# The leaky activation of the first three segments, written in place in its PSUM bank

## The chip, the cores and the metric

The kernel runs on one core of one Trainium2 chip. The metric is the device time of one execution in microseconds (us), lower is better. Engines are named as the profile names them: PE (TensorE matmul), PEld (its weight loads), DVE (VectorE), ACT (ScalarE), POOL (GpSimd), SP (SyncE, which here only issues DMAs).

## The reference, cut to what matters

A decayed linear attention produces `x` of 3072 tokens by 512. Two feed-forward layers follow, each 512 to 2048 to 512; the first has a leaky activation, the second `h * cos(h)`:

```
h = x @ w_in                       # 3072x512 @ 512x2048
g = np.maximum(0.01 * h, h)
x = g @ w_out                      # 3072x2048 @ 2048x512
h = x @ w_in2 ;  g = h * np.cos(h) ;  out = g @ w_out2
```

The change touches only the way from `h` to `g` of the first layer.

## The kernel before

**Numbers in two parts.** Every float32 operand of a matmul is held as a high part, rounded to the matmul's input format, and a low part, the rest. A product is three matmuls that add up in one PSUM bank (`mm3`, lines 361 to 364): high by high, low by high, high by low. So each intermediate is split: a copy on ACT makes the high part (`high_g`, line 568), a subtraction on DVE makes the low part (`low_g`, line 572).

**Tiling of the first layer.** Tokens come in six blocks of 512. The hidden width of 2048 comes in 16 chunks `f` of 128. For one block and one chunk, `gemm1` (line 550) makes one *product* `hp`: 12 matmuls into one whole PSUM bank of 128 by 512 float32. `Leaky.begin` (line 558) applies the leaky activation (Prelu on ACT, line 560) and writes it to the tile `t` in SBUF, of which there are two. `high_g` and `low_g` read `t` and write the pair `g` (three buffers). `gemm2_a` (line 782) then adds `g` times the second weight into four accumulators `acc`: 12 matmuls more. This text calls them the *accumulation* of that product.

**Segments.** The weights of the first layer have to be rounded on the chip before use, so the first two blocks are cut into four segments: block 0 chunks 0 to 6, block 1 chunks 0 to 3, block 0 chunks 7 to 15, block 1 chunks 4 to 15; then blocks 2 to 5 whole. The first three segments have 7 + 4 + 9 = 20 products; this text numbers them 0 to 19 in their order, and product 20 is the first of the fourth segment.

**Banks.** Products rotate through a pool of two PSUM banks (`ps_h`, `bufs=2`): product i takes the bank of product i-2. The accumulators hold four banks, attention the other two.

**The order of work** is written out by hand in the loop over `f` and kept by every engine's queue. In the iteration of product i come: `gemm1` of i on PE; `high_g` of i-1 on ACT; steps of attention (`slots`); perhaps a *rounding step* of the weights (`tick(0)`); the accumulation of product i-3 on PE (`second`), with the copies out of the accumulators where a segment ends; `low_g` of i-1 on DVE; the Prelu of i on ACT; attention again; perhaps a second rounding step (`tick(1)`).

A rounding step (`Weights.pieces`) is on ACT two activations (lines 121, 123) and a copy (line 142); on DVE a clamp (line 126), a shift (line 129), a bit merge (line 134) and the subtraction of the low part (line 145); on POOL one addition (line 139). `TICKS` says how many steps, none to two, an iteration gets. Attention's part on DVE is mostly the masking of scores (`sf`, line 489) and the scaling of its result (lines 524 and 528).

```
    ps_h = ctx.enter_context(tc.tile_pool(name="ps_h", bufs=2, space=PSUM))
...
        return tmp.tile([P, BLK], F32, tag=tag, name=tag, bufs=4 if tag == "o" else 2)
```

Of the kernel before, what the change touches and what calls it, by code (L numbers as in the profile page):

```python
# [81 lines left out]
def body(ctx: ExitStack, tc: tile.TileContext, att, w1, w2, tab, out):  # L82
# [19 lines left out]
    def stage(tag="o"):  # L102
        return tmp.tile([P, BLK], F32, tag=tag, name=tag, bufs=4 if tag == "o" else 2)
# [43 lines left out]
    class Weights:  # L147
# [52 lines left out]
        def tick(self):  # L200

            self.step()
            while self.run:
                self.step()
# [31 lines left out]
    def flush():  # L236
        for out, in_ in late:
            nc.sync.dma_start(out=out, in_=in_)
        del late[:]
# [112 lines left out]
    def load_wi(p, place):  # L352
        assert ("p", p) in made
        for old in [o for o in wi if wi[o][1] == place]:
            del wi[old]
        t = xpool.tile([P, 4096], F32R, tag=f"b{place}", name=f"b{place}")
        wi[p] = t, place
        for lo, hi in ((0, 1024), (1024, 2048), (2048, 3072), (3072, WIN)):
            nc.sync.dma_start(out=t[:, lo:hi].bitcast(F32), in_=w2i[p][:, lo:hi])
# [190 lines left out]
    def gemm1(key, f, x, hp):  # L550
        w = wslot[key, f, 0]
        xh, xl = x
        for k in range(KD):
            mm3(hp, w[:, k * P : k * P + P], w[:, 512 + k * P : 512 + k * P + P], xh[:, k, :], xl[:, k, :], k == 0, k == KD - 1)


    class Leaky:
        def begin(self, hp):
            t = stage("t")
            nc.scalar.activation(out=t, in_=hp, func=AF.Prelu, alpha=0.01)  # L560
            return (t,)

# [3 lines left out]
    def high_g(g, pair=None):  # L566
        pair = pair or gpool.tile([P, 2, BLK], F32R, tag="g", name="g")
        nc.scalar.copy(out=pair[:, 0], in_=g)  # L568
        return pair

    def low_g(g, pair, eng):
        eng.tensor_tensor(out=pair[:, 1], in0=g, in1=pair[:, 0].bitcast(F32), op=ALU.subtract)  # L572
        return pair

    with tc.manual_schedule():

        with ExitStack() as pctx, ExitStack() as actx:
# [70 lines left out]
            def half(f):  # L648
                nonlocal m, turn
                t = own(2 + turn % 2)  # L650
                turn += 1
                first, mid, last = rounding(raw2, t)
                high, low = parts(t, w2d[f], 0, nc.gpsimd, False, ostage)
                for i, step in zip((0, 2, 3, 3, 4, 5), (begin(f, 1), first, mid, last, high, low)):
                    agenda.put(m + i, step)
                agenda.put(m + 5, done("w", f))
                m += 3
# [25 lines left out]
            def pair(p):  # L683
                nonlocal m, turn
                t1, t2 = own(2 + turn % 2), own(3 - turn % 2)
                fetches = [begin(2 * p + i, 0) for i in range(2)]
                times = (0, 2, 3, 3, 3, 5, 6, 6, 4, 5, 7, 8, 8, 9, 9, 10, 10)
                pair_at(agenda, m, p, t1, t2, (raw2, raw2), fetches, times, (nc.gpsimd, nc.gpsimd, nc.vector), ostage, ostage, True)
                m += 9
# [8 lines left out]
            def last_pairs(ppool):  # L698
                def room(tag, n, dt, bufs):
                    return ppool.tile([P, n], dt, tag=tag, name=tag, bufs=bufs)  # L700

                def pout(n):
                    return room("po", 512, F32, 3)[:, :n]

                for i, p in enumerate(range(OWN, NF // 2)):
                    t1, t2 = late_fn(partial(room, "t1", 512, I32, 3)), late_fn(partial(room, "t2", 512, I32, 3))
                    raws = [late_fn(partial(room, "raw", 1024, I32, 3)) for _ in range(2)]
                    fetches = [lambda raw=raw, f=2 * p + j: fetch2(raw(), f, 0) for j, raw in enumerate(raws)]
                    times = (-2 if i else 0, 2, 3, 4, 1, 4, 5, 6, 5, 6, 7, 8, 8, 9, 9, 10, 10)
                    pair_at(agenda, LAST + 6 * i, p, t1, t2, raws, fetches, times, (nc.gpsimd, nc.gpsimd, nc.vector), pout, ostage)  # L710
# [8 lines left out]
            def load_w(n):  # L719
                for at in loads[:n]:  # L720
                    wa.load(*at)
                del loads[:n]

            def need(w, f, part):
                while (w.key, f, part) not in wslot:
                    load_w(1)
                    w.tick()
# [83 lines left out]
            def second(limit):  # L811
                while len(pending) > limit:
                    fn, *args = pending.pop(0)
                    fn(*args)
# [5 lines left out]
            leaky = Leaky()  # L820
            for seg, (n, f0, f1) in enumerate(SEGMENTS):
                limit = LAG - 2 if seg < 4 else 1
                steps = list(PLAN[seg])
                size, at = len(steps), 0

                def slots(k):
                    for _ in range(size - len(steps), min(size, (k * size + size // 2) // (2 * (f1 - f0)))):
                        steps.pop(0)()

                def tick(k):  # L830
                    if seg < 4 and wa.busy() and k < int(TICKS[seg][f - f0]):
                        if loads and (seg > 0 or loads[0][0] < NF - 7):
                            load_w(1)
                        wa.tick()
                    if n > 1:
                        flush()
                        agenda.run(2 * (NF * (n - 2) + f - START) + k)

                for f in range(f0, f1):
                    if n == NB - 1 and f % 4 > 1:  # L840
                        hp = ps_att.tile([P, 512], F32, tag="attA" if f % 4 == 2 else "attB", name="hp")
                    else:
                        hp = ps_h.tile([P, 512], F32, tag="h", name="hp")
                    hp = hp[:, :BLK]
                    if len(pending) > limit:
                        need(wa, pending[0][2], 1)
                    need(wa, f, 0)
                    gemm1("a", f, xs[n], hp)
                    if n == NB - 1 and f == 8:
                        load_wi(0, 0)  # L850
                    if n == NB - 1 and f == NF - 1:
                        load_wi(1, 1)
                    if prev:
                        g = leaky.finish(*begun)
                        gh = high_g(g)
                    slots(2 * (f - f0) + 1)
                    tick(0)
                    second(limit)
                    if prev:
                        pending.append((gemm2_a, *prev[:2], low_g(g, gh, nc.vector), *prev[2:]))  # L860
                    begun = leaky.begin(hp)
                    slots(2 * (f - f0) + 2)
                    tick(1)
                    prev = n, f, f0, f1
                if f1 == NF:
                    xs.pop(n)
                if n == NB - 2:
                    actx.close()
                    ppool = pctx.enter_context(tc.tile_pool(name="ppool", bufs=1))
                    last_pairs(ppool)  # L870
# [124 lines left out]
        for q in range(QUADS):  # L995
# [12 lines left out]
            if q == 0:  # L1008
                t = leaky.finish(*begun)
# [69 lines left out]
```

## Time and profile before

| | us |
|---|---|
| median of 3 runs | 1144.34 (1143.41 to 1146.3) |
| the profiled execution's own time | 1144.19 |
| its span in the trace | 1142.4 |
| PE busy in the span | 1118.1 (98%) |
| DVE busy in the span | 829.5 (73%) |

The profiled execution lies within 0.15 us of the median, and its span 1.8 us below its own time. The page's chain of the work that ended last puts 84% of the span on PE and 8% on DVE. The shares of the whole span say little on the first 160 us, in which the first three segments lie: there DVE is as full as PE, and the views by stretch and in order of time are needed. In them a row's duration counts from the start of an instruction to its end; neighbours on one engine overlap by some 0.08 us, and the matmuls of a product start every 0.23 us though each is shown at 0.39 us.

### The profile page before, as it was taken

Reading aid. Unit: us, or ns where it says so; the run is one execution under the profiler, and the core shown is the slowest. Engines: PE = TensorE matmul, PEld = TensorE weight load, DVE = VectorE, ACT = ScalarE, POOL = GpSimd, SP = SyncE. Lnnn points to the kernel's source line nnn. Section 1 sums busy time; section 2 is a strip of 40 time slices with the busy share of each in tenths; the row PEclk is TensorE's granted clock in tenths of the full one; section 3 lists DMA queues with packets and bytes.
Section 4 is the critical chain, followed back from the end, with each engine's and each line's share of the span. In section 5 each row is a group of like instructions: output and inputs, shape, how many; then the busy total and the mean of one; then the engine's idle time right before and its main releaser. Section 6 shows DMA issues by size and latency. Waiting matters only on the chain.

```text
span 1142.4 us, 15590 instructions
## 1 busy us (share of the span) xinstructions
PE 1118.1 (98%) x5584; PEld 924.7 (81%) x5584; DVE 829.5 (73%) x1334; ACT 524.9 (46%) x954; POOL 272.0 (24%) x253
## 2 busy tenths in 40 slices
PE   7889999999999999999999989999999999999998
PEld 5678888888888888788888868888888888888886
DVE  7899975344465465655298698798797897867875
ACT  5457643333454444444355445444454453444432
POOL 5455432222344445344166100000000000000000
PEclk9999999999999999999999999999999999999999
DMA  9906422223344444543477456558448366433312
GB/s 342 333 2 219 168 74 74 75 74 119 122 167 156 160 158 153 175 127 107 142 267 299 154 200 209 181 204 314 157 166 285 121 240 230 141 127 139 134 69 75
DMA packets 73806, 190.14 MB, mean 166 GB/s; under 512 B 8192, under 2 KB 12416, under 8 KB 73728
## 3 DMA queue, kind: packets, MB, share of 16 engines
q1 hardware_dynamic: 73584, 188.88, 47.7%
q8 instruction: 44, 0.72, 0.2%
q14 instruction: 34, 0.28, 0.1%
q10 hardware_dynamic: 144, 0.26, 0.1%
HBM read 136.68 MB, written 52.43 MB: 166 GB/s over the span
## 4 chain that ended last, share of the span: by engine, by line
PE 84%; DVE 8%; ACT 3%; DMA 2%; POOL 2%; issue 2%; ACTq 0%; POOLq 0%; DVEq 0%; SPq 0%
PE hp L364 11%; PE hp L362 11%; PE hp L363 10%; PE acc L362 10%; PE acc L363 10%; PE acc L364 10%; PE attB L364 4%; PE attB L362 4%; PE attB L363 4%; PE attA L362 2%; PE attA L364 2%; PE attA L363 2%; PE attA L513 1%; POOL cbuf L139 1%; DVE w L145 1%
## 5 line engine op out<-in xcount | busy, mean ns | idle before, releaser
L362 PE MATMUL acc<-g,w 128*128 128x512 f32 x384 | 151.8, 395 | 0.8 <-DVE o L775 0.8
L364 PE MATMUL hp<-b,w 128*128 128x512 f32 x384 | 150.1, 391 | 1.2 <-POOL b L540 1.1
L362 PE MATMUL hp<-b,w 128*128 128x512 f32 x384 | 150.2, 391 | 0.5 <-ACT b L539 0.5
L363 PE MATMUL acc<-g,w 128*128 128x512 f32 x384 | 149.9, 390 | 0.3 <-DVE w L145 0.3
L363 PE MATMUL hp<-b,w 128*128 128x512 f32 x384 | 149.8, 390 | 0.0
L364 PE MATMUL acc<-g,w 128*128 128x512 f32 x384 | 149.7, 390 | 0.0
L917 ACT ACTIVATE r<-r,bias 128x512 f32<-128x512 f32 x96 | 69.6, 725 | 88.0 <-DVE r L916 88.0
L572 DVE TENSOR_TENSOR g<-t,g 128x512 fp32r<-128x512 f32 x96 | 95.8, 1000 | 16.0 <-ACT g L568 15.4
L362 PE MATMUL hp<-w,b 128*128 128x512 f32 x224 | 87.4, 390 | 0.8 <-DVE c L898 0.8
L363 PE MATMUL hp<-w,b 128*128 128x512 f32 x224 | 87.2, 389 | 0.0
L364 PE MATMUL hp<-w,b 128*128 128x512 f32 x224 | 87.2, 389 | 0.0
L364 PEld LDWEIGHTS hp<-b,w 128*128 128x128 f32 x384 | 72.1, 188 | 17.4 <-POOL b L540 2.5
L362 PEld LDWEIGHTS acc<-g,w 128*128 128x128 f32 x384 | 72.1, 188 | 16.7 <-DVE o L775 1.3
L362 PEld LDWEIGHTS hp<-b,w 128*128 128x128 f32 x384 | 72.1, 188 | 15.7 <-ACT b L539 0.8
L364 PEld LDWEIGHTS acc<-g,w 128*128 128x128 f32 x384 | 72.1, 188 | 15.3
L363 PEld LDWEIGHTS hp<-b,w 128*128 128x128 f32 x384 | 72.1, 188 | 14.5 <-DVE w L145 0.2
L363 PEld LDWEIGHTS acc<-g,w 128*128 128x128 f32 x384 | 72.1, 188 | 14.2 <-DVE w L145 0.6
L457 DVE TENSOR_TENSOR qbd<-raw,qbd 64x256 fp32r<-64x256 f32 x64 | 49.8, 777 | 37.4 <-ACT qbd L456 36.3
L363 PE MATMUL acc<-w,g 128*128 128x512 f32 x192 | 75.1, 391 | 1.1 <-DVE g L572 1.0
L364 PE MATMUL acc<-w,g 128*128 128x512 f32 x192 | 74.8, 389 | 0.0
L362 PE MATMUL acc<-w,g 128*128 128x512 f32 x192 | 74.7, 389 | 0.0
L568 ACT CAST g<-t 128x512 fp32r<-128x512 f32 x96 | 59.3, 618 | 33.3 <-PE acc L364 32.3
(194 smaller groups left out, 2462.9 us busy)
## 6 DMA issues: line engine op xcount, KB each, us to landing
b<-w2i SPq DMA_DIRECT2D x60, 512.0 KB, 5.9
w<-w SPq DMA_DIRECT2D x32, 512.0 KB, 7.7
raw<-att SPq DMA_DIRECT2D x32, 512.0 KB, 4.8
w<-w2d SPq DMA_DIRECT2D x32, 512.0 KB, 7.9
w<-xq SPq DMA_DIRECT2D x28, 512.0 KB, 6.1
cbuf<-w SPq DMA_DIRECT2D x24, 512.0 KB, 3.8
xq<-o SPq DMA_DIRECT2D x40, 256.0 KB, 2.3
w2i<-o SPq DMA_DIRECT2D x32, 256.0 KB, 2.8
```

What stands on the lines that cost most here:

```text
L139: nc.gpsimd.tensor_tensor(out=t, in0=t, in1=raw[:, :, 0], op=ALU.add)
L145: nc.vector.tensor_tensor(out=w[:, 512:1024], in0=t.bitcast(F32), in1=w[:, 0:512].bitcast(F32), op=ALU.subtract)
L362: nc.tensor.matmul(o, sh, mh, start=start, stop=False)
L363: nc.tensor.matmul(o, sl, mh, start=False, stop=False)
L364: nc.tensor.matmul(o, sh, ml, start=False, stop=stop)
L457: nc.vector.tensor_tensor(out=ql[rows, :, cols], in0=rq[rows], in1=qh[rows, :, cols].bitcast(F32), op=ALU.subtract)
L513: nc.tensor.matmul(po[r * D : r * D + D, h // 2, :], d["vp"][:, h, :], s, start=c == 0, stop=c == 0 or h > 1)
L568: nc.scalar.copy(out=pair[:, 0], in_=g)
L572: eng.tensor_tensor(out=pair[:, 1], in0=g, in1=pair[:, 0].bitcast(F32), op=ALU.subtract)
L917: nc.scalar.activation(out=r, in_=r, func=AF.Sin, bias=bias[:, 1:2], scale=1.0)
```

## The change

In the first three segments `Leaky.begin` no longer takes a tile `t` from SBUF: the Prelu writes its result over `hp` in the product's PSUM bank, and `high_g` and `low_g` read it from there. From the fourth segment on nothing changes.

```diff
     class Leaky:
-        def begin(self, hp):
-            t = stage("t")
+        def begin(self, hp, stay=False):
+            t = hp if stay else stage("t")
             nc.scalar.activation(out=t, in_=hp, func=AF.Prelu, alpha=0.01)
             return (t,)
...
-                    begun = leaky.begin(hp)
+                    begun = leaky.begin(hp, seg < 3)
```

No instruction is added, removed or moved on any engine. What differs is operands and waits. On ACT, in the iteration of product 0 (`w_0_166` is attention's result on its way to the block `b`, `hp` the product), the Prelu and the copy of the high part stand where they stood:

```order
 L142 CAST w_0_476<-cbuf 128x512 [waits Pool_49]
 L539 CAST b_508<-w_0_166 128x2x128 [waits DVE_49]
-L560 ACTIVATE t<-hp 128x512 [waits PE_49]
-L568 CAST g<-t 128x512 [waits Activation_49]
+L560 ACTIVATE hp<-hp 128x512 [waits PE_49]
+L568 CAST g<-hp 128x512 [waits Activation_49]
 L539 CAST b_508<-w_0_166 128x2x128 [waits DVE_49]
```

Only the tile has changed. On PE, at the start of product 2 (`w_0_476` is the first weight of chunk 2), behind attention's matmuls:

```order
 L502 MATMUL attB<-w_0_154,st 128x128
 L513 MATMUL attB<-sf,vp 64x128 x4
-L362 MATMUL hp<-b_248,w_0_476 128x512 [waits Activation_49]
+L362 MATMUL hp<-b_248,w_0_476 128x512 [waits DVE_49,Activation_49]
 L363 MATMUL hp<-b_248,w_0_476 128x512
 L364 MATMUL hp<-b_248,w_0_476 128x512
```

The first matmul of product 2 waited for the Prelu of product 0, the last reader of its bank. Now it waits for DVE, and the DVE instruction that the semaphore's value stands for is the subtraction of the low part of product 0. The same holds for products 3 to 20, each with the low part of the product two before. One more thing differs in the built program: product 21, of the fourth segment, is placed in the bank of product 20, where it waits for the Prelu of product 20; before, it had the other bank. From product 22 on the two banks alternate again.

## Rows read from the trace of the kernel before

**Rows 1.** The page, the span:
```profile
span 1142.4 us, 15590 instructions
```
**Rows 2.** Busy time by stretch; columns as the head line says:
```profile
core 0: us, PE busy (x) PEld busy (x) DVE busy (x) ACT busy (x) POOL busy (x), PEclk, DMA share, GB/s
60.00:90.00 30.00, 26.38 (x153) 20.90 (x152) 29.32 (x48) 17.15 (x33) 15.09 (x12) 1.00 0.08 26
90.00:120.00 30.00, 30.00 (x134) 24.85 (x133) 29.36 (x42) 21.92 (x40) 15.45 (x14) 1.00 0.52 186
```
**Rows 3.** Groups between 30 and 160 us: count, busy us, mean ns, idle before:
```profile
L572 DVE TENSOR_TENSOR g<-t,g 128x512 fp32r<-128x512 f32 x19 | 27.4, 1445 | 0.0
L560 ACT ACTIVATE t<-hp 128x512 f32<-128x512 f32 x20 | 11.9, 594 | 2.6 <-DVE g L572 2.6
L489 DVE TENSOR_TENSOR sf<-attA,tb 128x512 f32<-128x512 f32 x9 | 6.2, 688 | 1.2 <-PE attA L486 1.1
```
**Rows 4.** In order of time, POOL and DVE: start us, duration us, engine, line:
```profile
88.05 1.78 POOL L139 TENSOR_TENSOR cbuf<-cbuf,w 128x512 int32<-128x512 int32 x1 [1.55 <-DVE cbuf L134]
88.58 1.81 DVE L572 TENSOR_TENSOR g<-t,g 128x512 fp32r<-128x512 f32 x1
...
95.67 1.80 DVE L572 TENSOR_TENSOR g<-t,g 128x512 fp32r<-128x512 f32 x1
...
147.20 1.64 POOL L139 TENSOR_TENSOR cbuf<-cbuf,w 128x512 int32<-128x512 int32 x1 [2.21 <-DVE cbuf L134]
147.59 0.68 DVE L489 TENSOR_TENSOR sf<-attB,tb 128x512 f32<-128x512 f32 x1
148.19 0.94 DVE L126 TENSOR_SCALAR cbuf<-cbuf 128x512 f32<-128x512 f32 x1
```
**Rows 5.** PE in order of time: products 2, 3, 5, 6, and three waits:
```profile
43.47 0.50 PE L362 MATMUL hp<-b,w 128*128 128x512 f32 x1
...
47.50 1.13 PE L486 MATMUL attA<-w,w 128*128 128x256 f32 x4 [1.01 <-DVE sf L489]
...
49.59 0.50 PE L362 MATMUL hp<-b,w 128*128 128x512 f32 x1
...
56.33 1.13 PE L486 MATMUL attA<-w,w 128*128 128x256 f32 x4 [1.00 <-DVE sf L489]
...
65.60 0.49 PE L362 MATMUL hp<-b,w 128*128 128x512 f32 x1
...
71.89 1.13 PE L486 MATMUL attA<-w,w 128*128 128x256 f32 x4 [3.12 <-DVE sf L489]
...
77.12 0.39 PE L362 MATMUL hp<-b,w 128*128 128x512 f32 x1
```
**Rows 6.** DVE in order of time: low parts 0, 1, 3 and 4:
```profile
46.04 0.68 DVE L572 TENSOR_TENSOR g<-t,g 128x512 fp32r<-128x512 f32 x1
...
53.88 1.80 DVE L572 TENSOR_TENSOR g<-t,g 128x512 fp32r<-128x512 f32 x1
...
69.34 1.77 DVE L572 TENSOR_TENSOR g<-t,g 128x512 fp32r<-128x512 f32 x1
...
80.14 1.79 DVE L572 TENSOR_TENSOR g<-t,g 128x512 fp32r<-128x512 f32 x1
```
**Rows 7.** Products 10 and 11 on PE; DVE's copies as the first segment ends:
```profile
101.21 0.39 PE L362 MATMUL hp<-b,w 128*128 128x512 f32 x1
...
102.86 1.29 DVE L775 COPY o<-acc 128x512 f32<-128x512 f32 x2
...
106.65 0.39 PE L362 MATMUL hp<-b,w 128*128 128x512 f32 x1
```
**Rows 8.** DVE in the iteration of product 13: masking, and low part 12:
```profile
121.17 0.69 DVE L489 TENSOR_TENSOR sf<-attA,tb 128x512 f32<-128x512 f32 x1
...
125.10 0.68 DVE L572 TENSOR_TENSOR g<-t,g 128x512 fp32r<-128x512 f32 x1
```
**Rows 9.** The fourth segment: product 21 on PE, Prelu of product 20:
```profile
165.14 0.39 PE L362 MATMUL hp<-b,w 128*128 128x512 f32 x1
...
166.28 0.59 ACT L560 ACTIVATE t<-hp 128x512 f32<-128x512 f32 x1
```

## The prediction

> **What bounds the kernel now.** I read the span first [rows 1]: 1142.4 us, against 1144.19 us of the execution's own time, so 1.8 us lie around it and are left alone by the change. Next the busy time by stretch [rows 2], because the change ends with product 19, in the first 160 us. In the stretch from 60 us PE lacks 3.6 of 30 us and DVE lacks 0.7; from 90 us on PE is full and DVE still lacks only 0.6. So DVE binds up to about 86 us, and PE behind that, with DVE hard on its heels. The PEclk column is 1.00 in both, the upper of the two levels (2.4 GHz); I expect no price from the clock.
>
> The third view is the groups by line [rows 3]. The subtraction of the low part (L572) has a mean of 1445 ns, while the masking of scores (L489), of the same 128 by 512 elements, has 688. The view in order of time tells why [rows 4]. POOL's addition starts at 88.05 and ends at 89.83; the low part starts at 88.58 and ends at 90.39, some 0.6 us behind POOL: it was held until POOL was done. At 147.59 a masking runs inside a POOL addition (147.20 to 148.84) and takes 0.68 us, unheld. The masking reads one operand from PSUM, the low part reads both from SBUF. The clamp behind the masking, SBUF to SBUF, is held again (0.94 us, ending 0.3 us behind POOL).
>
> The fourth view is PE in order of time beside DVE [rows 5, 6]. It shows when low part i ends and when PE starts product i+2. Before the change those two are strangers. Now the second waits for the first.
>
> **The change part by part.** *Low parts.* After the change the low part reads `hp` from PSUM, as the masking does, so I take 0.68 us for it where it was 1.8. 19 times (1445 - 680) ns are 14.5 us of holding, some 13 low parts at 1.1 us. Not all of it comes back: where the next DVE instruction is a clamp it is held in the low part's place, and ends 0.3 us behind POOL instead of 0.6 + 0.4 behind, a gain of 0.6. Where the next is a masking the whole 1.1 us is gained. The bounds are 0 (held as before) and 1.1; the row at 147.59 is the nearest, as it has the same shape, engine and operands.
>
> *Prelu and high part.* No row shows ACT or DVE writing PSUM. The nearest rows are the Prelu from PSUM to SBUF, 594 ns, and, on the other engine, 688 ns [rows 3]. A tenth of a us either way, 20 times, is at most 2 us if all of it lay on the path; ACT is not on it while DVE is late, so I take 0 and keep 2 us either way for the range. The tile `t` itself cost one wait of 2.6 us on ACT [rows 3], off the path.
>
> *The bank's wait.* Product i+2 must now wait for low part i. On PE nothing passes a waiting matmul: the accumulation behind it and attention's scores are queued there, and DVE waits for those in turn. I work the rows forward [rows 5, 6], carrying PE's delay:
> - Product 2 started at 43.47; low part 0 ends at 46.04 + 0.68 = 46.72. Wait 3.25, delay 3.25.
> - Product 3 started at 49.59, behind a wait of 1.01 for a masking, which is now long done: ready at 49.59 + 3.25 - 1.01 = 51.83. Low part 1 ends at 53.88 + 0.68 = 54.56. Wait 2.7, delay 5.0.
> - The wait of 1.00 at 56.33 goes too: delay 4.0 at product 4, which finds its bank free.
> - Product 5: ready at 65.60 + 4.0 = 69.6; low part 3 ends at 69.34 + 0.68 = 70.0. Wait 0.4, delay 4.4. I give DVE no gain so far: the 1.1 us it saved at low part 1 it spends waiting for the later scores.
> - The wait of 3.12 at 71.89 goes. Product 6: ready at 77.12 + 4.4 - 3.1 = 78.4; low part 4, now 1.1 us earlier by the relief at low part 3, ends at 80.14 - 1.1 + 0.68 = 79.7. Wait 1.3, delay 2.6.
>
> So the first stage costs 7.7 us of waits and gives back 5.1: **+2.6**. Behind it PE was full, and every wait adds whole.
>
> *Ends of segments.* DVE copies two of the four accumulators out, and the next low part is queued behind these copies. Product 10 now waits for low part 8, which waits for the second copy, which waits for PE's last matmul before product 10. That bubble is one copy and one low part: 1.29 / 2 + 0.68 and a tenth for the handing over, **+1.4** [rows 6, 7]. What hid it before was that low part 8 was not due for two more products. In the iteration of product 13 the same queue begins with a masking that waits for PE's scores after product 13. From that masking to the end of low part 12 DVE needs 125.78 - 121.17 = 4.6 us [rows 8], most of it a rounding step. PE has one accumulation to do meanwhile, half of the 5.44 us between products 10 and 11 [rows 7], 2.7 us. **+1.9** at product 14.
>
> *Iterations with two rounding steps.* From 88.58 to 95.67 DVE needs 7.09 us [rows 4], after the relief some 6.5; PE needs 5.44. With no lead DVE makes PE wait 1.0 there, and iterations with one step or none give the lead back. Some four places are of that kind; I put **+0.6** for all, an estimate between 0 and 3.
>
> *The swapped bank.* Product 21 waits for the Prelu of product 20. Before, it started at 165.14, and that Prelu ended at 166.28 + 0.59 = 166.87 [rows 9]. PE and ACT come to this place equally late, so **+1.7**.
>
> The sum is 2.6 + 1.4 + 1.9 + 0.6 + 1.7 = 8.2 us. What comes behind is bound by PE and hides none of it.
>
> Two banks are all that products have, and rows 5 and 6 show PE ready 0.4 to 3.3 us before the low part that now frees one. The Trainium skill ("PSUM — Partial Sum Buffer", Summary: rules for kernel authors) says to evacuate PSUM promptly, which speaks against this change. By that rule alone there would be the waits without relief on DVE, and the time would be that of the third rival below; by rows 4 the relief is real, and the sum stays at 8.2.
>
> **The rivals.**
> *Slower by 8, the forecast*: 1144.2 + 8.2 = 1152.4 us.
> *Faster.* The mechanism is DVE's relief up to 86 us: PE's three waits for the masking (5.1 us) go and the bank is never waited for, 1144.2 - 5.1 = 1139 us. For it speaks that DVE binds there and is held 1.1 us at a time; it decides at the point where low part i ends before PE is ready for product i+2. Against it: at products 2 and 3 the low part is 3.3 and 2.7 us too late, and the relief of low part 0 is nothing (0.68 already).
> *No change to measure.* The first stage costs its 2.6, but then DVE, some 0.6 us per product ahead, keeps a lead through both ends of segments, and Prelu 20 comes earlier too: 1144.2 + 2.6 = 1146.8 us. Against it: at both ends DVE waits for PE's own matmuls, which no lead shortens.
> *Slower by 16.* Reading `hp` is held by POOL like reading `t`: 13 low parts at 0.6 us are not gained, 1152.4 + 7.8 = 1160 us. Against it stands the masking at 147.59.
>
> **How the numbers follow.** About 0.3% (3.4 us) is what a measurement of this kernel tells from no change. Chances: forecast 0.72, faster 0.07, no change 0.14, slower by 16 0.07. The forecast's own range is 1148 to 1158: the 2 us for ACT's writes, 0 to 3 for the double steps instead of 0.6, and a handing over of 0.1 to 0.3 us at each of some eight waits. The whole range adds half of the no-change case below, to 1146; the faster case and the one slower by 16 stay outside. So faster 0.07, the same 0.14, slower 0.79. I predict 1152.5 us; the median of the runs is 0.15 us above the profiled execution, which changes nothing.
>
> **What would show it.** In the profile after: the mean of L572 between 30 and 160 us near 700 ns, and the clamp (L126) held more often. PE idle before products 2, 3 and 6 for some 3, 3 and 1 us with DVE's L572 as releaser, and no more waits of PE for L489 at the places that now read 47.50, 56.33 and 71.89. Near products 10 and 14 PE idle for 1.4 and 1.9 us behind DVE's copies; at product 21 an idle of 1.7 us put down to ACT's Prelu. The prediction is wrong if PE starts product 3 within a us of 49.6, or if L572 keeps durations of 1.8.

## The result, and the profile after

The changed kernel takes 1154.96 us (median of 4 runs, 1154.47 to 1155.44), the kernel before 1144.64 beside it. The ratio is 1.0085, with a 95% interval of 1.0073 to 1.0097: slower by 10.3 us, where 8.2 had been forecast.

The page of after: the span, and the busy time of each engine.

```profile
span 1153.5 us, 15598 instructions
...
PE 1123.8 (97%) x5584; PEld 928.7 (81%) x5584; DVE 818.5 (71%) x1334; ACT 524.2 (45%) x954; POOL 269.7 (23%) x253
```

The span is longer by 11.1 us than that of [rows 1], while DVE works 11.0 us less than before (829.5). The change took work off an engine and lost time all the same. The page counts 8 instructions more in all than [rows 1]; on each engine above the number is that of before.

Busy time by stretch, after, with the columns of [rows 2]:

```profile
30.00:60.00 30.00, 26.05 (x155) 20.87 (x150) 26.80 (x48) 15.78 (x35) 14.87 (x14) 0.89 0.87 298
60.00:90.00 30.00, 27.48 (x172) 22.19 (x171) 24.60 (x46) 15.17 (x29) 13.57 (x11) 1.00 0.09 28
90.00:120.00 30.00, 28.38 (x125) 22.85 (x124) 28.19 (x42) 21.76 (x40) 16.03 (x14) 1.00 0.52 183
120.00:150.00 30.00, 28.04 (x118) 22.51 (x117) 23.95 (x38) 19.00 (x36) 11.09 (x8) 0.94 0.47 158
```

From 60 to 90 us DVE is no longer full: 24.6 us where it was 29.3. From 90 us on PE, which was full, lacks 1.6 us and then 2.0 us in 30. And the granted clock, 1.00 before, is 0.89 and 0.94 in two of these stretches. Of that more below.

Groups by line in the first stages (30 to 167 us), after:

```profile
L126 DVE TENSOR_SCALAR cbuf<-cbuf 128x512 f32<-128x512 f32 x28 | 23.5, 840 | 0.1
...
L572 DVE TENSOR_TENSOR g<-hp,g 128x512 fp32r<-128x512 f32 x19 | 13.0, 684 | 3.4 <-ACT g L568 3.4
...
L560 ACT ACTIVATE hp<-hp 128x512 f32<-128x512 f32 x20 | 11.6, 581 | 7.1 <-PE hp L364 7.1
```

and the clamp before:

```profile
L126 DVE TENSOR_SCALAR cbuf<-cbuf 128x512 f32<-128x512 f32 x29 | 21.9, 754 | 0.2
```

The low part (L572) now takes 684 ns every time, against 1445 in [rows 3]: with one operand in PSUM POOL no longer holds it. The clamp behind it takes 840 instead of 754, so 28 x 0.086 = 2.4 us of the 14.4 that the low parts are spared (27.4 - 13.0) are held again in another place. ACT's writing into PSUM costs nothing that shows: the Prelu takes 581 ns, 594 in [rows 3].

What PE waited for between 30 and 190 us, after (line, releaser: us in total, times, longest):

```profile
PE hp L362 <- DVE g L572: 10.7, 8, 3.6
PE hp L362 <- ACT t L560: 1.6, 1, 1.6
```

No product waited for either before; the three waits for the masking of [rows 5], 5.1 us, are gone.

### The profile page after: what moved, and what is told of

Its sections match the earlier page's. It is cut to its first block, busy times and chain, and to the rows that moved or that the text cites. A ratio compares the mean times of both kernels' runs of the same rounds, so it can differ in the third digit from the quotient of the medians.

```text
span 1153.5 us, 15598 instructions
## 1 busy us (share of the span) xinstructions
PE 1123.8 (97%) x5584; PEld 928.7 (81%) x5584; DVE 818.5 (71%) x1334; ACT 524.2 (45%) x954; POOL 269.7 (23%) x253
## 4 chain that ended last, share of the span: by engine, by line
PE 83%; DVE 8%; DMA 4%; ACT 2%; issue 1%; POOL 1%; SPq 0%; ACTq 0%; DVEq 0%; POOLq 0%
PE hp L362 11%; PE hp L364 11%; PE hp L363 11%; PE acc L362 10%; PE acc L363 10%; PE acc L364 10%; PE attB L364 4%; PE attB L362 4%; PE attB L363 4%; PE attA L362 2%; PE attA L364 2%; PE attA L363 2%; DMA w<-w 1%; DMA w<-att 1%; PE attA L513 1%
## 5 line engine op out<-in xcount | busy, mean ns | idle before, releaser
L362 PE MATMUL hp<-b,w 128*128 128x512 f32 x384 | 152.3, 397 | 12.3 <-DVE g L572 10.7
L364 PE MATMUL hp<-b,w 128*128 128x512 f32 x384 | 151.5, 395 | 0.0
L363 PE MATMUL hp<-b,w 128*128 128x512 f32 x384 | 151.3, 394 | 0.0
L362 PEld LDWEIGHTS hp<-b,w 128*128 128x128 f32 x384 | 72.9, 190 | 30.4 <-issue 6.7
L364 PEld LDWEIGHTS hp<-b,w 128*128 128x128 f32 x384 | 73.1, 190 | 15.8 <-POOL b L540 0.4
L363 PEld LDWEIGHTS hp<-b,w 128*128 128x128 f32 x384 | 73.0, 190 | 14.4
L572 DVE TENSOR_TENSOR g<-t,g 128x512 fp32r<-128x512 f32 x76 | 66.1, 870 | 16.6 <-ACT g L568 16.0
L362 PE MATMUL attB<-w,w 128*128 128x512 f32 x180 | 70.4, 391 | 0.5 <-DVE w L966 0.5
```

The lines of the kernel that those rows point to most:

```text
L362: nc.tensor.matmul(o, sh, mh, start=start, stop=False)
L363: nc.tensor.matmul(o, sl, mh, start=False, stop=False)
L364: nc.tensor.matmul(o, sh, ml, start=False, stop=stop)
```

## Experiments

Each run is compared with runs of the kernel before on the same chip. "Faster" and "slower" below are against their median unless another kernel is named.

**The changed kernel again.** Its first profile had stretches at a lower clock, so I wanted a second one.

> The changed kernel once more, unaltered. Theory (the clock's fall behind the idle of 1.96 us at product 14 is there in some executions and not in others, and costs 0.8 us net, since the small waits behind it take up the rest): 1154.5 to 1155.4 us; if product 14 now takes 3.0 us, products 15 and 17 wait some 0.2 us each instead. Rival (it falls every time in this kernel): product 14 takes 4.4 us again.

1154.98 us (1154.44 to 1155.78), ratio 1.0086 [1.0072, 1.01]. The two runs at a mean granted clock of 0.999 took 1154.45 and 1154.44, the two at 0.994 took 1155.78 and 1155.52. Its profile, of the 1154.45 one, is the cleanest picture of the change and is called the clean one below; only from 30 to 60 us is its granted clock under 1.00, at 0.94. The products at which PE now waits, products 2, 3, 5, 6, 10, 11, 14, 15, 17, 18 and 21, without a wait products 8, 13, 20 and 22, and the last matmul ahead of product 15 (start us, duration us, engine, line, operation, idle before and its releaser):

```profile
47.12 0.77 PE L362 MATMUL hp<-b,w 128*128 128x512 f32 x1 [3.56 <-DVE g L572]
...
54.83 0.47 PE L362 MATMUL hp<-b,w 128*128 128x512 f32 x1 [1.41 <-DVE g L572]
...
70.42 0.47 PE L362 MATMUL hp<-b,w 128*128 128x512 f32 x1 [0.83 <-DVE g L572]
...
80.18 0.47 PE L362 MATMUL hp<-b,w 128*128 128x512 f32 x1 [1.68 <-DVE g L572]
...
92.67 0.39 PE L362 MATMUL hp<-b,w 128*128 128x512 f32 x1
...
105.09 0.50 PE L362 MATMUL hp<-b,w 128*128 128x512 f32 x1 [1.38 <-DVE g L572]
...
111.06 0.50 PE L362 MATMUL hp<-b,w 128*128 128x512 f32 x1 [0.24 <-DVE g L572]
...
122.09 0.39 PE L362 MATMUL hp<-b,w 128*128 128x512 f32 x1
...
130.40 0.50 PE L362 MATMUL hp<-b,w 128*128 128x512 f32 x1 [1.96 <-DVE g L572]
...
135.76 0.39 PE L364 MATMUL acc<-g,w 128*128 128x512 f32 x1
...
136.36 0.50 PE L362 MATMUL hp<-b,w 128*128 128x512 f32 x1 [0.22 <-DVE g L572]
...
147.82 0.47 PE L362 MATMUL hp<-b,w 128*128 128x512 f32 x1 [0.27 <-DVE g L572]
...
155.12 0.47 PE L362 MATMUL hp<-b,w 128*128 128x512 f32 x1 [0.86 <-DVE g L572]
...
166.13 0.39 PE L362 MATMUL hp<-b,w 128*128 128x512 f32 x1
...
175.96 0.50 PE L362 MATMUL hp<-b,w 128*128 128x512 f32 x1 [1.62 <-ACT t L560]
...
182.28 0.39 PE L362 MATMUL hp<-b,w 128*128 128x512 f32 x1
```

and products 8, 13, 14, 20 and 22 before:

```profile
90.33 0.39 PE L362 MATMUL hp<-b,w 128*128 128x512 f32 x1
...
117.53 0.39 PE L362 MATMUL hp<-b,w 128*128 128x512 f32 x1
...
123.71 0.39 PE L362 MATMUL hp<-b,w 128*128 128x512 f32 x1
...
157.09 0.39 PE L362 MATMUL hp<-b,w 128*128 128x512 f32 x1
...
171.90 0.39 PE L362 MATMUL hp<-b,w 128*128 128x512 f32 x1
```

The differences of these starts are the terms of the sum; they are compared with the forecast further down.

**A third bank.** The decisive question: is in-place work itself dear, or only the bank that it holds?

```diff
+                    if shared:
+                        accs[n].append(accs[n][0])
...
+                    elif seg < 3 and (f - f0 + (0, 7, 11)[seg]) % 3 == 2:
+                        hp = ps_acc.tile([P, 512], F32, tag="acc3", name="hp")
...
-                    begun = leaky.begin(hp, seg < 3)
+                    begun = leaky.begin(hp, seg < 3 and (seg, f) != (2, NF - 1))
```

> The changed kernel with product 19 through t, and with a third bank for the products of the first three segments, used for every third of them. The bank is taken from the fourth quarter of the accumulation: in these segments that quarter is added into the bank of the first quarter, the same matmuls and copies with another sum in it. Theory (the loss is the wait for a bank, the relief of VectorE is a gain by itself): PE's waits for L572 are gone, the three waits for L489 stay gone, the clock stays up, 1139 to 1143 us, faster than the kernel before. Rival (reading and writing PSUM in place costs time by itself, whatever the banks): 1150 to 1153 us.

> Control of the run before it: the kernel before, with the same third bank and the same sharing of the first quarter's bank, and t in SBUF. Both theories: no product waited for a bank in these segments, so 1144.5 us, within 1. If it moves by more, the sharing itself has a price, and the run with three banks is to be read against this one.

Both kernels leave out a separate sum for the fourth quarter of the accumulation: it is added into the bank of the first, so their output is not that of the layer. They measure time alone, with as many instructions on each engine as before. In place with three banks takes 1142.32 us, ratio 0.9975 [0.9966, 0.9984]: faster than the kernel before by 2.6 us. The control takes 1145.97, 1.0007 [0.9998, 1.0016]: sharing an accumulator's bank costs up to a microsecond or two, where a segment ends. Against the control, in place with a third bank gains 3.65 us. PE's waits, first in place, then the control:

```profile
PE attA L486 <- DVE sf L489: 3.0, 2, 2.0
```

```profile
PE attA L486 <- DVE sf L489: 5.1, 3, 3.1
PE acc L362 <- ACT o L773: 1.3, 1, 1.3
```

No product waits for a low part any more. The control's wait of 1.3 us for an accumulator's bank (L773) comes of the sharing and is absent in place, so a part of the 3.65 us may be that wait; the relief alone is worth 2.6 to 3.65 us. The expectation had two things wrong. The clock did not stay up in the profiled execution (0.94 from 60 to 90 us). And the waits for the masking do not vanish. DVE's relief shortens them by 2.1 us of 5.1. In the changed kernel they vanish because PE comes later, having waited for its bank.

**The hold without the relief.** One column of the product is copied out behind each low part, so that the bank is held as long; `t` stays in SBUF.

```diff
+                        if held is not None:
+                            nc.vector.tensor_copy(out=sink[:, 0:1], in_=held[:, 0:1])
+                    held = hp if seg < 3 else None
```

> The kernel before, t in SBUF, with one more instruction behind each low part of the first three segments: VectorE copies one column of the product out of its bank, so that the bank is held just as long as by the change, and the low part keeps both operands in SBUF. Theory (the change is a hold that costs and a relief that gives back): the hold without the relief, slower than the changed kernel by the 0.6 us at each of some 13 low parts, 1160 to 1163 us; L572 keeps a mean near 1400 ns. Rival (the relief is worth nothing): 1155 us, as the changed kernel.

1165.71 us, ratio 1.0187 [1.017, 1.0204], 10.7 us behind the changed kernel and more than I expected. Groups, and what PE waited for:

```profile
L572 DVE TENSOR_TENSOR g<-t,g 128x512 fp32r<-128x512 f32 x17 | 22.6, 1330 | 0.0
...
L863 DVE COPY sink<-hp 128x1 f32<-128x1 f32 x16 | 2.4, 149 | 0.1
```

```profile
PE hp L362 <- DVE sink L863: 15.0, 7, 3.6
PE hp L362 <- ACT w L142: 5.2, 4, 2.1
```

The low part is held as before. PE waits 20 us in eleven places, 15.0 of it put down to the copied column. At the other four a rounded weight (L142) comes last, but there too the column's copy ends no more than 0.1 us ahead of it (product 11: 119.95 against 120.05), so the bank alone would have held PE nearly as long. The probe itself costs DVE 20 x 0.149 = 3.0 us, and the mean granted clock of its runs, 0.991 to 0.996, is a little lower, so 10.7 is an upper bound of what the relief gives back; the forecast's 7.8 lies below it. Both runs together show the change as two effects of opposite sign on one engine: a hold that costs, and a relief that pays less than the hold costs.

**Parts of the change.** In place in the first segment only, then in the second and third only:

```diff
-                    begun = leaky.begin(hp, seg < 3)
+                    begun = leaky.begin(hp, seg < 1)
```

```diff
-                    begun = leaky.begin(hp, seg < 3)
+                    begun = leaky.begin(hp, 0 < seg < 3)
```

> In place only in the first segment (products 0 to 6). By the terms measured in the trace of after: the first stage alone, +2.3 us, 1146.9 us; a swap of the banks falls at products 7 and 8, where PE is not ready sooner. If the ends of the segments (products 10 and 14) cost what they cost by themselves, this run has none of them. Rival (the terms are not separate: what the first segment leaves of lead decides the later waits): above 1149 or below 1145 us.

> In place only in the second and third segments (products 7 to 19). By the terms of the trace of after: 1.4 at product 10, 2.0 at product 14, 1.7 of slow clock behind it, 1.7 at the swap, some 1 to 1.5 in small waits: +8, 1152 to 1153 us. Rival (these waits come only since the first segment used up VectorE's lead): +2 to +4, 1147 to 1149 us.

1146.40 us (1.0009 [1.0, 1.0018]) and 1154.73 us (1.0085 [1.0071, 1.0099]), that is +1.1 and +9.4; their sum, 10.5, is near the whole change (10.3). The second one is above its expectation, and its trace says why: in the first segment, where this kernel is the kernel before, it stands as follows, with products 8 and 14 below.

```profile
72.34 2.08 PE L486 MATMUL attA<-w,w 128*128 128x256 f32 x4 [3.14 <-DVE sf L489]
...
80.38 0.39 PE L362 MATMUL hp<-b,w 128*128 128x512 f32 x1
...
92.78 0.39 PE L362 MATMUL hp<-b,w 128*128 128x512 f32 x1
...
130.53 0.50 PE L362 MATMUL hp<-b,w 128*128 128x512 f32 x1 [1.96 <-DVE g L572]
...
131.34 0.40 PE L362 MATMUL hp<-b,w 128*128 128x512 f32 x1
```

Behind the old wait for the masking the four matmuls of L486 take 2.08 us, not the 1.13 of [rows 5], and product 6 starts 3.3 us later than before. That is the clock (0.89 from 60 to 90 us), and it is not of the change. At product 8 this execution is still 2.4 us behind the kernel before (92.78 against 90.33, shown above); of the 10.6 us by which its span (1153.0) exceeds [rows 1], 8.2 come behind that product. In the clean trace of after it is 10.3 - 2.3 = 8.0. The first-segment run's span (1144.7) exceeds [rows 1] by 2.3, what the clean trace has at product 8. So the traces show that the parts are separate; the medians alone do not, since one of them has the clock's price in a segment that the change leaves alone. In the first-segment run the wait of 3.14 us does not exist, which I take to be why it is only +1.1 by the medians: among the runs of before there will be executions that pay for this wait in clock. That isn't shown.

**The swapped bank.** Product 19 alone goes through `t` again, and the two banks alternate.

```diff
-                    begun = leaky.begin(hp, seg < 3)
+                    begun = leaky.begin(hp, seg < 3 and (seg, f) != (2, NF - 1))
```

> The changed kernel, but product 19, the last of the third segment, still goes through t, so that the two banks of the products alternate without a swap. Theory of the swapped bank: product 21 no longer waits for the Prelu of product 20, about 1.7 us are gone, 1153.3 us against 1154.96 of the changed kernel. Rival: PE only waits at another place behind it and the swap is worth nothing, 1155.0 us.

1152.98 us (1152.38 to 1153.93), 2.0 us below the changed kernel; 1.7 was expected. In its trace product 21 waits for nothing and starts 8.06 us after product 20, as before the change (165.14 - 157.09 = 8.05); in the clean trace of after it is 9.83 (175.96 - 166.13).

**The ends of the segments.** If products 8 and 12 are not in place, products 10 and 14 need not wait for a low part. The first segment and product 19 are not in place here either.

```diff
-                    begun = leaky.begin(hp, seg < 3)
+                    begun = leaky.begin(hp, 0 < seg < 3 and (seg, f) not in ((1, 1), (2, 8), (2, NF - 1)))
```

> In place only in the second and third segments, as one run before, but without products 8, 12 and 19: product 10 then waits for no low part, nor does product 14, and the banks are not swapped. What is left is the term of the iterations with two rounding steps, forecast at 0.6 us (range 0 to 3); in the run with all of these two segments in place the small waits at products 11 to 18 added up to some 3 us. Theory (the small waits are a price of their own): 2 to 3.5 us, 1147 to 1148.5 us. First rival (they only come since the waits at products 10 and 14 used up VectorE's lead; without those the forecast of 0.6 is right): 1145 to 1146 us. Second rival (the waits at the ends of segments only move one product on, to products 11 and 15): +5 or more, 1150 us.

1155.06 us, 1.0085 [1.0071, 1.0099]: nothing gained against the second and third segments whole (1154.73), though the swap, worth 2.0 us, is gone as well. That is the second rival, which had put the loss at 5 us or more. Products 10, 11 and 15, with a later matmul of product 11:

```profile
103.64 0.39 PE L362 MATMUL hp<-b,w 128*128 128x512 f32 x1
...
111.16 0.50 PE L362 MATMUL hp<-b,w 128*128 128x512 f32 x1 [1.92 <-DVE g L572]
...
112.66 0.63 PE L362 MATMUL hp<-b,w 128*128 128x512 f32 x1
...
138.06 0.50 PE L362 MATMUL hp<-b,w 128*128 128x512 f32 x1 [2.49 <-DVE g L572]
```

The waits of 1.38 and 1.96 us at products 10 and 14 (14 waits for nothing here either) have become 1.92 and 2.49 at products 11 and 15. The clock takes a part too: product 11 falls to 0.63 us a matmul, and the first segment has 0.89 from 60 to 90 us, as in the run with the second and third segments. DVE is late by its queue of copies at a segment's end; whichever product next needs a bank that DVE must free pays for it. The run therefore says nothing on the size of the small waits by themselves, for which I had made it.

**The clock at product 14.** In the first profile of after product 14 ran slowly behind its wait:

```profile
130.32 0.50 PE L362 MATMUL hp<-b,w 128*128 128x512 f32 x1 [1.96 <-DVE g L572]
...
132.22 0.63 PE L362 MATMUL hp<-b,w 128*128 128x512 f32 x1
...
137.51 0.39 PE L362 MATMUL hp<-b,w 128*128 128x512 f32 x1
```

Matmuls of 0.63 us instead of 0.39, and 7.19 us to product 15, against 5.96 in the clean profile. To see whether the idle is the cause I filled it:

```diff
+                    if (seg, f) == (2, 10):
+                        fill = ps_att.tile([P, 512], F32, tag="attB", name="fill")
+                        for k in range(FILL):
+                            nc.tensor.matmul(fill, wslot["a", 7, 0][:, :P], xs[n][0][:, 0, :], start=True, stop=True)
```

> The changed kernel with nine more matmuls of 128 by 512 elements ahead of product 14, into a bank that is free there; their result is read by nobody. They run in PE's wait of 1.96 us. Theory (the 4.44 us of product 14 instead of 2.72 are the clock that fell to the lower level because PE stood still): product 14 takes 2.7 us, the granted clock between 120 and 150 us is 1.00, and the time falls by 1.7 us to 1153.3. Rival (product 14 is long for another reason, or the clock falls all the same): 1155 us or more.

1155.10 us: no gain, the expectation was wrong. In its profile (`FILL` is 9; the lines of this kernel lie one lower) the filler takes the place of the wait. The granted clock is 1.00 from 120 to 150 us, and product 14 runs at full clock:

```profile
128.87 2.20 PE L852 MATMUL fill<-b,w 128*128 128x512 f32 x9
131.00 0.50 PE L363 MATMUL hp<-b,w 128*128 128x512 f32 x1
```

but the clean profile of the changed kernel and the run with the second and third segments have full clock there behind the same 1.96 us of idle. So this run doesn't show that the filler did it. What it shows is that the slow product 14 is worth less than the 1.7 us I had read off it: the clean profile of after gets 1.2 us earlier to product 15 and then waits 0.22 and 0.27 at products 15 and 17, so that at product 20 (166.13 against 166.85) 0.7 are left.

**Another order on DVE.** PE's waits for the masking can be shortened without holding a bank: in the kernel before, the low part of the first segment is put behind attention's steps.

```diff
-                    if prev:
+                    late_low = seg == 0
+                    if prev and not late_low:
...
                     slots(2 * (f - f0) + 2)
+                    if prev and late_low:
+                        pending.append((gemm2_a, *prev[:2], low_g(g, gh, nc.vector), *prev[2:]))
```

> The kernel before, t in SBUF, with one step of the first segment in another place: the low part (L572) stands on VectorE behind attention's steps of that iteration instead of ahead of them. Theory (the three waits of 1.01, 1.00 and 3.12 us of PE for the masking come from the held low part ahead of it): the masking starts 1.4 to 1.8 us earlier, the waits shrink by 0.6, 1.0 and 1.1 us, 1141.5 to 1142.5 us, faster than the kernel before. Rival (VectorE has the same work to do up to 86 us, and the low part that is now late makes PE wait in the accumulation instead): 1144.5 us or more.

> The kernel before, with the low part behind attention's steps in all of the first three segments, not in the first alone (that gave 1140.5 us). Theory (TensorE is full from 86 us on, so that the order on VectorE decides nothing there): 1140.5 us, within 0.7. Rival (the second and third segments gain too, at the waits behind 86 us): 1139.5 or less. Rival (the later low part makes the accumulation wait): 1142 us or more.

1140.49 us, ratio 0.996 [0.9948, 0.9973], and in all three segments (`seg < 3`) 1140.18, 0.9959 [0.9945, 0.9972]: faster than both kernels, the first by at least a microsecond more than expected, and not told apart from each other. POOL, DVE and PE at the place of the largest wait, first segment only, and its low parts between 30 and 160 us:

```profile
66.84 1.60 POOL L139 TENSOR_TENSOR cbuf<-cbuf,w 128x512 int32<-128x512 int32 x1 [1.15 <-DVE cbuf L134]
...
67.33 0.69 DVE L489 TENSOR_TENSOR sf<-attA,tb 128x512 f32<-128x512 f32 x1
...
68.08 1.13 PE L486 MATMUL attA<-w,w 128*128 128x256 f32 x4 [0.74 <-DVE sf L489]
...
69.81 0.68 DVE L572 TENSOR_TENSOR g<-t,g 128x512 fp32r<-128x512 f32 x1
...
L572 DVE TENSOR_TENSOR g<-t,g 128x512 fp32r<-128x512 f32 x19 | 26.4, 1392 | 0.1
```

The masking runs inside POOL's addition unheld, and by the time the low part comes POOL is through: it takes 0.68 us, where the one of [rows 6] at 69.34 took 1.77. PE's wait there is 0.74 instead of 3.12. On the whole the low parts are held nearly as before, 1392 ns on average against 1445: what this kernel gains is that PE's masking no longer stands behind a held one. Against the median of before on its chip (1145.33) it gains 4.8 us; the two traces, both at a clock of 1.000, differ by 3.4 (spans 1139.0 and 1142.4). The rest may be what the runs of before pay in clock, which isn't shown.

## Why the prediction was right, and by how much it was off

The sign, the place and the mechanism held: PE now waits for DVE's low parts, the relief is real and too small. The time lies inside the range, 2.5 us above the value. Clean trace of after against the trace of before, as differences of the starts of products:

| step | forecast | measured | from |
|---|---|---|---|
| first stage, to product 8 | +2.6 | +2.3 | 92.67 - 90.33 |
| product 10 | +1.4 | +1.5 | 105.09 - 101.21, less 2.34 |
| product 14 | +1.9 | +2.1 | 130.40 - 123.71, less (122.09 - 117.53) |
| the rest up to product 20 | +0.6 | +3.0 | 166.13 - 157.09 = 9.04, less the three above |
| swapped bank | +1.7 | +1.3 | 182.28 - 171.90 = 10.38, less 9.04 |
| sum | +8.2 | +10.3 | spans 1152.7 - 1142.4 |

*Low parts: right.* 0.68 us was taken, 684 ns came; the clamps are held more (0.086 us each). This is also what the Trainium skill says ("SBUF — State Buffer", section "Who interferes with whom"): a DVE instruction with two SBUF inputs contends with a GpSimd instruction that reads SBUF, one with at most one SBUF input does not, unless it runs in one of the two-port modes. The rows of the low part agree: 1445 ns with both operands in SBUF, 684 with one. The clamp has a single SBUF input and is held all the same (840 ns); whether it runs in such a mode no run here shows.

*First stage: the path right, the last tenths by luck.* Forecast waits were 3.25, 2.7, 0.4 and 1.3 at products 2, 3, 5 and 6; shown are 3.56, 1.41, 0.83 and 1.68. The short one, at product 3, is the clock again: product 2 starts with matmuls of 0.77 us and runs slowly, and what it loses product 3 need not wait. The waits for the masking went, as forecast. At product 6, where the forecast's path ends, the delay is 80.18 - 77.12 = 3.1 us for 2.6. The +2.3 at product 8 needs a gain that the forecast has not: product 7 stood still before, for attention's low part on POOL (`b`, L540), and no longer does.

```profile
86.55 0.50 PE L364 MATMUL hp<-b,w 128*128 128x512 f32 x1 [0.50 <-POOL b L540]
```

*Ends of segments: right*, 1.38 and 1.96 shown for 1.4 and 1.9. One reading in the working was wrong without harm: of the 4.6 us on DVE from the masking to the end of low part 12, a rounding step is 2.2 and not most.

*Iterations with two rounding steps: the term that failed*, 3.0 us instead of 0.6, the upper end of its range. I had taken DVE and PE as equal but for some small deficit that other iterations give back. The places were right: between the low part that each of these four products waits for and the one before it, DVE has two rounding steps (`TICKS`). The rows show four waits, 0.24, 0.22, 0.27 and 0.86 us at products 11, 15, 17 and 18: 1.6 us, nothing given back. The other 1.4 are the handing over, which I had put in the range and not in the value. It comes in two pieces, both to be read in the rows. Matmuls start every 0.23 us, but idle is counted from the shown end 0.39 us after a start: product 15 could have followed the row at 135.76 at 135.99, it starts at 136.36, 0.37 late, of which the row calls 0.22 a wait. That is 0.16 for each wait. And a product whose first matmul has waited needs about 0.14 longer (first matmul 0.50 us instead of 0.39), which shows at the start of the next. For these four waits and the two at the ends, 4 x 0.16 + 6 x 0.14 = 1.5.

*Swapped bank: right*, 1.62 us of wait, less 0.44 given back by product 22; the run without the swap is 2.0 us faster.

*"I expect no price from the clock": wrong as a statement, cheap in effect.* The clock does fall behind the new idles, in some executions; it costs 1.1 to 1.3 us between runs of the changed kernel (1155.78 and 1155.52 against 1154.45). But the kernel before pays at its own wait of 3.12 us, so that the difference between the two kernels is 10.2 us at their highest clocks too (1154.45 at 0.999, 1144.27 at 1.0).

*The rivals.* "Faster" was priced too high even for a kernel that never waits for its bank: with three banks the relief gave 2.6 us against the kernel before and 3.65 against the control, not 5.1. "No change" needed DVE's lead to cover what follows the first stage; the table has 1.5, 2.1 and 3.0 us there, nothing of it covered. "Slower by 16" named the relief as the deciding thing; the run that holds without relief, at +20.8 with its probe, shows that it is. That run is also what the rule of the Trainium skill to evacuate PSUM promptly ("PSUM — Partial Sum Buffer", "Summary: rules for kernel authors") comes to here when nothing is given back; the trace agrees with the rule, which has no price.

What stays open: whether the fall of the clock behind an idle of some 2 us could be kept away by other work on PE, and what the small waits would be if those at the ends were really gone.

## What to carry to other kernels

An operation moved into PSUM to spare SBUF traffic also prolongs the life of its bank. Before such a change, set the end of the last reader of the bank against the time at which TensorE wants it back, in the trace and product by product; here that forecast three of the large waits (1.38, 1.96 and 1.62 us) within 0.1 us. If PE waits because POOL holds DVE, look first at whether the held instruction could stand elsewhere in the queue: moving it behind the one that PE waits for gave 4.8 us by the medians, 3.4 by the traces, and needed no bank. And where a dependency is added at many places with no slack, add some 0.3 us for each hand-over, on top of the idle that the view shows.

## What was not expected of the hardware

The granted clock of TensorE fell to the lower of its two levels (matmuls of 0.63 us instead of 0.39, starting every 0.43 us instead of 0.23) behind idles as short as 1.92 us (product 11 of the run that spares the ends) and 1.96 us (product 14 of the first profile of after), and did not behind 1.96 us at the same place in two other profiles. Behind the wait of 3.12 us the kernel before kept its clock in the execution shown in [rows 5], and the run with the second and third segments did not, behind 3.14. So the fall is a matter of the execution, not of the length of the idle alone. It would explain a part of the spread of the kernel before, 1143.4 to 1146.6 us in all its runs at mean clocks of 1.0 to 0.996: in the kernel with the low part moved in the first segment, whose longest wait of PE between 30 and 190 us is 0.74 us, five runs lie between 1140.34 and 1140.74, at clocks of 0.998 to 1.0. It can't explain all of it: with the low part moved in three segments five runs spread from 1139.74 to 1141.69 at clocks of 0.999 and 1.0, and the kernel before has 1144.72 and 1146.62 at the same 0.996.
